# Start reordered, two chunks masked by products, six weight pieces rounded on GpSimd instead of thirteen

## The chip, the core and the metric

The kernel runs on one core of a Trainium2 chip. The core has five engines that each work through their own list in order: TensorE (PE, matrix products), VectorE (DVE), ScalarE (ACT), GpSimd (POOL) and SyncE (SP), which here issues every transfer. An instruction waits until what it needs is there, and whatever stands behind it on its engine waits with it. The metric is the device time of one execution in microseconds, as the median of the runs shown.

## The reference

Three stages follow one another on 3072 tokens (4 batches of 768) of width 256. The first is a chunked linear attention with decay, in chunks of 32 tokens:

```python
for c in range(seq // chunk):
    cum = np.cumsum(log_a[:, :, sl], axis=-1)
    L = np.exp(cum[..., :, None] - cum[..., None, :]) * causal
    M = einsum('bhin,bhjn->bhij', C, B) * L
    y[:, :, sl] = einsum('bhij,bhjd->bhid', M, x) + einsum('bhin,bhnd->bhid', C, state) * exp(cum)
    state = decay_full * state + sum(B x decay_from_j)
...
g = relu(x @ w_in) ** 2          # 256 -> 2048
x = g @ w_out                    # 2048 -> 256
...
h = (x @ w1) * (x @ w2) @ w3     # 256 -> 1024 -> 1024
out = h @ w_out                  # 1024 -> 256
```

## The kernel before

The tokens go through in tiles of 512. A tile's two feed-forward stages are phases: A (the squared relu) has 16 steps m, B the bilinear one. The order of phases is A0, A1, B0, B1 and on. The attention of a tile, five or six chunks g in units u of a few chunks, is put into slots of the phase before; only the first tile's (chunks 0 to 5, units 0 to 2) stands alone ahead of A0, in an order that is written out by hand in `startup`.

Products keep float32 accuracy by three passes: each operand is split into a high part, rounded (on ScalarE, or for weights on GpSimd), and a low part (VectorE, `split_lo`, L141), and six matmuls of 128x512 make one product. A step m of phase A is `h_mm` (first product, L816), relu (L830) and square (L838 on ScalarE or L840 on VectorE), the high part of gp (ScalarE, L846), its low part (VectorE, L141), and the second product into acc (TensorE, L863), which comes one or two steps after the first one. Names in the rows follow these tiles: mm for first products, tmp, gp, acc, xt for the attention's result, which is the operand of the next phase A.

While A0 runs, the 16 weight pieces "a" arrive (ua) and are converted: `conv_words` on ScalarE (L196, L198), `conv_bits` on VectorE (L207, L210), and `conv_parts`, which makes wa: the high part by a cast on ScalarE (L230) for pieces 0 to 2 and on GpSimd (L228) for the others, and the low part on VectorE. Pieces of the later weights (uo, cv, wo, wo2l and u3) follow on the same lines.

In the attention a chunk's e (exponentials of decays) is made by `unit_e1` on TensorE and ScalarE for units 0 to 3, from the products of `pick` (L665). For units 0 to 2 the causal mask is added by a product of ident and nmask (L660). For unit 3, which is chunks 6 and 7, `chunk_mask` cuts it afterwards with an affine select on GpSimd (L556), as it does for the chunks after them. `chunk_g` multiplies e by g (VectorE, L621), `chunk_y` makes y on TensorE (L752), the state is updated by L714, and `chunk_hand` copies it on as xb (L721). `unit_split` splits B and C of a unit, writes them to memory (hl_d) and `unit_bc` reads them back as bt and cb.

Buffers decide what waits. The pool gp has four places that are used in turn by pick (twice), zero, the gp tiles of the steps m, and the tile hl of a unit's split when it is given no other place, which is so for unit 5:

```python
def new_gp():
    return gp.tile([P, 2, 512], F32R, tag="gp", name="gp")
...
hl = wts.tile([P, 2, 512], F32R, tag=place, name="hl") if place else new_gp()
```

A tile that takes over a place waits until the readers of the former tile are done, transfers too. A transfer counts as done when it has landed. SP's transfers use eight semaphores in turn (DMAHW0 to 7), so each also waits until the one eight places ahead of it has landed. The matmuls that make up a step are emitted by a planner that sets the order on each engine by costs and by due slots; outside `startup` that order is not written down anywhere in the code.

## Time and profile before

| what | before |
|---|---|
| median of 3 runs | 561.94 us (561.61 to 562.13) |
| profiled execution's own time | 561.75 us |
| span of its records | 560.0 us |
| TensorE busy | 546.9 us, 98% of the span |
| VectorE, ScalarE, GpSimd busy | 361.9, 288.7, 88.6 us |
| granted TensorE clock over the span | 0.996 of full |
| transfers | 59.49 MB |

Times of rows are counted from the start of the span. TensorE's share is an average: the first 90 us, with the first tile's attention and the conversion of weights, are looser than the rest. Nearly all of the stalls of the run lie there and in the move to the next phases.

### The profile page before, as it was taken

The page shows a single profiled execution, that of the slowest core. Times are in us where ns is not written, and L with a number is a line of the kernel's source. Part 1 is how long each engine was busy: PE and PEld are TensorE (multiplying, and loading weights), DVE is VectorE, ACT ScalarE, POOL GpSimd, SP SyncE. Part 2 cuts the span into 40 slices and gives each one's busy share as a digit, 9 for nine tenths or more (in the row PEclk, how much of TensorE's full clock was granted, in tenths as well). Part 3 has the DMA queues.
Part 4 walks back from the last instruction along what each step waited for, and adds up shares of the span by engine and source line. Part 5 has one row for each costly group of instructions (what it writes and reads, how often), then busy time and mean ns, then how long its engine had stood idle before and what let it go on. Part 6 is the DMA issues. An engine that isn't in the chain of part 4 may idle for free.

```text
span 560.0 us, 9614 instructions
## 1 busy us (share of the span) xinstructions
PE 546.9 (98%) x3580; PEld 460.3 (82%) x3580; DVE 361.9 (65%) x655; ACT 288.7 (52%) x553; POOL 88.6 (16%) x136
## 2 busy tenths in 40 slices
PE   8979999999999999999999999999999999999997
PEld 6757777888888888888888888888888888888886
DVE  5799998977898555466476456474456574545431
ACT  6799768787884342444343444342535332544332
POOL 8264730000001240013030003020012010000000
PEclk9989999999999999999999999999999999999999
DMA  8797690253446470075250066020162220100001
GB/s 240 248 288 249 213 389 7 74 153 107 156 149 169 102 198 1 15 191 143 58 142 1 29 165 148 22 78 1 52 175 77 57 68 1 39 1 1 1 1 37
DMA packets 48735, 59.49 MB, mean 106 GB/s; under 512 B 22960, under 2 KB 36784, under 8 KB 48688
## 3 DMA queue, kind: packets, MB, share of 16 engines
q1 hardware_dynamic: 48688, 58.88, 35.5%
q8 instruction: 28, 0.46, 0.4%
q14 instruction: 19, 0.16, 0.1%
HBM read 50.20 MB, written 8.65 MB: 105 GB/s over the span
## 4 chain that ended last, share of the span: by engine, by line
PE 81%; DVE 8%; DMA 5%; ACT 3%; SPq 1%; issue 1%; DVEq 0%; ACTq 0%
PE mm L816 43%; PE acc L863 18%; PE acc L916 12%; PE mm L257 4%; PE y L752 2%; DVE gp L141 2%; PE g L615 2%; DMA hl_d<-gp 1%; DMA hl_d<-hl 1%; SPq L93 1%; DVE wa L141 1%; DMA raw<-in_raw_dram 1%; DVE cvs L207 1%; DMA u<-in_w_dram 1%; DVE cvs L210 1%
## 5 line engine op out<-in xcount | busy, mean ns | idle before, releaser
L816 PE MATMUL mm<-xt,wa 128*128 128x512 f32 x576 | 148.6, 396 | 3.2 <-DVE wa L141 2.0
L846 ACT CAST gp<-tmp 128x512 fp32r<-128x512 f32 x144 | 89.4, 621 | 115.3 <-DVE tmp L904 63.6
L863 PE MATMUL acc<-gp,wa 128*128 128x512 f32 x576 | 145.9, 392 | 1.3 <-DVE gp L141 0.7
L141 DVE TENSOR_TENSOR gp<-tmp,gp 128x512 fp32r<-128x512 f32 x144 | 103.6, 720 | 61.1 <-ACT gp L846 60.8
L816 PE MATMUL mm<-x,w 128*128 128x512 f32 x576 | 142.6, 393 | 0.0
L816 PEld LDWEIGHTS mm<-xt,wa 128*128 128x128 f32 x576 | 106.4, 190 | 25.8 <-ACT tmp L830 2.4
L863 PEld LDWEIGHTS acc<-gp,wa 128*128 128x128 f32 x576 | 106.5, 188 | 24.5 <-DVE gp L141 1.5
L816 PEld LDWEIGHTS mm<-x,w 128*128 128x128 f32 x576 | 104.5, 188 | 20.5 <-ACT tmp L896 0.2
L830 ACT ACTIVATE tmp<-mm 128x512 f32<-128x512 f32 x96 | 57.3, 596 | 50.8 <-PE mm L816 50.4
L916 PEld LDWEIGHTS acc<-w3o,gp 128*128 128x128 f32 x576 | 75.8, 190 | 4.6 <-DVE gp L141 0.3
L916 PE MATMUL acc<-w3o,gp 128*128 128x256 f32 x576 | 78.5, 283 | 0.1
L840 DVE TENSOR_TENSOR tmp<-tmp 128x512 f32<-128x512 f32 x68 | 47.5, 699 | 29.8 <-ACT tmp L830 28.5
L904 DVE TENSOR_TENSOR tmp<-tmp,mm 128x512 f32<-128x512 f32 x48 | 32.9, 686 | 48.5 <-PE mm L816 44.9
L556 POOL TENSOR_SCALAR_AFFINE_SELECT e<-e 96x768 f32<-96x768 f32 x26 | 25.8, 1005 | 235.8 <-DMA e<-e_d 228.7
L896 ACT COPY tmp<-mm 128x512 f32<-128x512 f32 x48 | 28.1, 586 | 45.9 <-PE mm L816 45.6
L575 POOL TENSOR_TENSOR xb<-xb,dec 96x256 f32<-96x256 f32 x32 | 23.1, 723 | 94.6 <-DMA xb<-in_xb_dram 93.6
L621 DVE TENSOR_TENSOR e<-g,e 128x384 f32<-128x384 f32 x52 | 27.6, 551 | 6.0 <-PE g L615 4.7
L257 PE MATMUL mm<-wo,w 128*128 128x256 f32 x128 | 23.7, 284 | 0.9 <-DVE w L141 0.9
L257 PEld LDWEIGHTS mm<-wo,w 128*128 128x128 f32 x128 | 20.6, 191 | 2.5 <-DVE w L141 1.5
L742 DVE SCALAR_TENSOR_TENSOR xb<-xb,through,y 32x64 f32<-32x64 f32 x72 | 20.4, 283 | 2.8 <-PE y L714 1.1
L615 PEld LDWEIGHTS g<-cb,bt 96*128 96x128 f32 x96 | 16.1, 190 | 2.8
L257 PE MATMUL mm<-wo2l,w 128*128 128x256 f32 x64 | 18.1, 283 | 0.0
(109 smaller groups left out, 447.2 us busy)
## 6 DMA issues: line engine op xcount, KB each, us to landing
u<-in_w_dram SPq DMA_DIRECT2D x24, 512.0 KB, 4.4
ua<-in_w_dram SPq DMA_DIRECT2D x16, 512.0 KB, 6.8
e<-e_d SPq DMA_DIRECT2D x40, 192.0 KB, 4.6
xb<-in_xb_dram SPq DMA_DIRECT2D x32, 192.0 KB, 3.7
bt<-hl_d SPq DMA_DIRECT2D x78, 48.0 KB, 2.0
hl_d<-gp SPq DMA_DIRECT2D x9, 384.0 KB, 2.5
cb<-hl_d SPq DMA_DIRECT2D x66, 48.0 KB, 2.0
out_dram<-tmp SPq DMA_DIRECT2D x10, 256.0 KB, 2.9
```

The costliest lines, as they stand in the source:

```text
L141: return nc.vector.tensor_tensor(out=lo, in0=src, in1=hi.bitcast(F32), op=ALU.subtract)
L257: nc.tensor.matmul(acc[:, :DM], v[:, l, e % 4 * P:(e % 4 + 1) * P], wo2[1 + e // 2][r][:, e % 2 * DM:(e % 2 + 1) * DM], start=(n == 0), st ...
L615: nc.tensor.matmul(ps[:, 2 * pp:2 * pp + 2], w, un["c2"][:, pr, :, j * CH:(j + 1) * CH], start=True, stop=True)
L621: nc.vector.tensor_tensor(out=m, in0=ps, in1=m, op=ALU.mult)
L816: i = nc.tensor.matmul(ps, w[m][:, l, col + k * P:col + (k + 1) * P], rhs[k][:, r, :], start=((l, r, k) == (1, 0, 0)), stop=((l, r, k) == ...
L830: nc.scalar.activation(r, ps, AF.Relu)
L840: nc.vector.tensor_tensor(out=g32, in0=r, in1=r, op=ALU.mult)
L846: nc.scalar.copy(g[:, 0, :], d[k])
L863: i = nc.tensor.matmul(acc["x2", t][e], wa[m][:, l, 256 + e * P:256 + (e + 1) * P], g[:, r, :], start=(m == 0 and n == 0), stop=(m == MF - ...
L896: nc.scalar.copy(s, ps)
L904: nc.vector.tensor_tensor(out=p32, in0=prods[t, m], in1=ps, op=ALU.mult)
L916: i = nc.tensor.matmul(acc["o"][sub // per][:, sub % per, :], g[:, l, sub * P:(sub + 1) * P], w3o[m // 2][:, r, m % 2, :], start=(m == 0 a ...
```

## The change

Four things are changed. The high part of pieces 9 to 15 is rounded on ScalarE and no longer on GpSimd. Chunks 6 and 7 are masked by the product of ident and nmask in `unit_e1`, in A0's slots 1 and 2, and no longer by `chunk_mask`. Since ident is then read during A0, it can't lie any longer where weight piece 9 will be put (wa9); it takes a place in the pool gp, after the two picks and ahead of zero. And in `startup` piece 0 is loaded ahead of chunks 4 and 5, its words are made ahead of state(2), its bits and unit 2's e, g0 and m0 come sooner.

```diff
--- before.py
+++ after.py
@@ -48,6 +48,7 @@
 NEVER = -30000.0
 WARM = 2
 CONV0 = 3
+HI_POOL = range(3, 9)
 TMPB = 6
 SQ_DVE = {0: (), 1: (3, 4, 5, 6)}
 GM_DVE = (0,)
@@ -224,7 +225,7 @@
             wo2.append(w)
             return
         w = wts.tile([P, 2, 512], F32R, tag=PLACE[j % 8] if kind == "3" else f"w{kind}{j}", name=f"w{kind}{j}")
-        if kind == "a" and j > 2:
+        if kind == "a" and j in HI_POOL:
             nc.gpsimd.tensor_copy(w[:, 0, :], v)
         else:
             nc.scalar.copy(w[:, 0, :], v)
@@ -276,7 +277,7 @@
     id2 = const.tile([P, 32], F32, name="id2")
     e_d = dram.tile([4, 2, 2, 8, H, CH], F32, name="e_d")
     pick = [gp.tile([P, H, P], F32R, tag="gp", name="pick") for k in range(2)]
-    ident = wts.tile([P, P], F32R, tag="wa9", name="ident")
+    ident = gp.tile([P, P], F32R, tag="gp", name="ident")
     nmask = act1.tile([P, P], F32R, tag="cmask", name="nmask")[:, :CH]
     m_rel = new_tmp()
     m_oth = new_tmp()
@@ -649,21 +650,20 @@
         for j, g in enumerate(UNITS[u]):
             es[g] = e[:, j] if u != 2 else None
 
-    def unit_e1(u, q, mask=True):
+    def unit_e1(u, q):
 
         if u not in e0:
             unit_e0(u)
         k, v = divmod(UNITS[u][0], 4)
         ps = new_mm()[:, :4 * CH]
         ph = ps.rearrange("p (h c) -> p h c", h=2)
-        if mask:
-            nc.tensor.matmul(
-                ps.rearrange("p (n i) -> p n i", n=4), ident, nmask.unsqueeze(1).to_broadcast([P, 4, CH]),
-                start=True, stop=False, skip_group_check=True,
-            )
+        nc.tensor.matmul(
+            ps.rearrange("p (n i) -> p n i", n=4), ident, nmask.unsqueeze(1).to_broadcast([P, 4, CH]),
+            start=True, stop=False, skip_group_check=True,
+        )
         for h in range(2):
             nc.tensor.matmul(
-                ph[:, h], pick[k][:, 2 * q + h], e_first[:, v:v + 2], start=not mask, stop=True, skip_group_check=True
+                ph[:, h], pick[k][:, 2 * q + h], e_first[:, v:v + 2], start=False, stop=True, skip_group_check=True
             )
         nc.scalar.activation(
             e0[u][q // 2][:, :, 2 * (q % 2):2 * (q % 2) + 2].rearrange("p j h i -> p h j i"),
@@ -1015,15 +1015,16 @@
         for j, s in enumerate(ASLOT):
             g = FIRST[1] + j
             put(ph, s, chunk_pre, g)
-            put(ph, s, chunk_mask, g)
+            if j > 1:
+                put(ph, s, chunk_mask, g)
             put(ph, s + 1, chunk_g, g, 0)
             put(ph, s + 1, chunk_g, g, 1)
             put(ph, s + 2, chunk_y, g)
         put(ph, 1, unit_bc, 4, BCPLACE)
         put(ph, 1, conv_load, 2)
         for s in range(2):
-            put(ph, 1 + s, unit_e1, 3, 2 * s, False)
-            put(ph, 1 + s, unit_e1, 3, 2 * s + 1, False)
+            put(ph, 1 + s, unit_e1, 3, 2 * s)
+            put(ph, 1 + s, unit_e1, 3, 2 * s + 1)
         put(ph, 4, unit_e, 4)
         put(ph, 7, unit_split, 5)
         put(ph, 10, unit_bc, 5)
@@ -1068,9 +1069,9 @@
         batch_load(1, 1, 3)
         chunk_xb(2)
         chunk_xb(3, "w124")
+        conv_load(1)
         chunk_xb(4, "w125")
         chunk_xb(5, "w126")
-        conv_load(1)
         unit_load(4)
         conv_load(2)
         picks, rounded = constants()
@@ -1107,6 +1108,7 @@
         unit_e1(1, 3)
         unit_pad(2)
         unit_g0(1)
+        conv_words(0)
         state(2)
         chunk_pre(4)
         m0(1)
@@ -1116,18 +1118,17 @@
         chunk_xb(6)
         unit_e1(2, 0)
         unit_e1(2, 1)
-        conv_words(0)
+        conv_bits(0)
+        unit_e1(2, 2)
         state(3)
+        unit_e1(2, 3)
+        unit_g0(2)
         chunk_pre(5)
         value(2)
-        unit_e1(2, 2)
-        unit_e1(2, 3)
-        conv_bits(0)
-        unit_g0(2)
+        m0(2)
         state(4)
         value(3)
         decays_e(0)
-        m0(2)
         conv_load(1)
         unit_load(5)
         conv_parts(0)
```

Three places show what this moves in the engines' lists. The first is ScalarE in the middle of A0, where the steps m6 and m7 get the high parts of their gp tiles (gp_938 and gp_983 before, gp_940 and gp_985 after; ua10 to ua12 are weight pieces, xb_541 takes over the state for one of the next chunks). Before:

```order
L846 CAST gp_938<-tmp_889 128x512 [waits Activation_49]
L196 ACTIVATE cvs_88<-ua11_632 128x512 [waits DMAHW3_49,DVE_49]
L198 ACTIVATE ua11_632<-ua11_632 128x512
L838 ACTIVATE tmp_936<-tmp_916 128x512 [waits Activation_49]
L144 CAST xt1_773<-y_105 128x96 [waits DVE_49]
L846 CAST gp_983<-tmp_936 128x512 [waits DMAHW2_49,DMAHW1_49,Activation_49]
L196 ACTIVATE cvs_87<-ua12_730 128x512 [waits DMAHW0_49,Pool_49]
L198 ACTIVATE ua12_730<-ua12_730 128x512
L721 COPY xb_541<-y_105 32x256 [waits DVE_49]
```

And after:

```order
L846 CAST gp_940<-tmp_891 128x512 [waits DMAHW2_49,DMAHW1_49,Activation_49]
L197 ACTIVATE cvs_88<-ua11_632 128x512 [waits DMAHW3_49,Pool_49]
L199 ACTIVATE ua11_632<-ua11_632 128x512
L838 ACTIVATE tmp_938<-tmp_918 128x512 [waits Activation_49]
L231 CAST wa9_902<-cvs_87 128x512 [waits DVE_49]
L721 COPY xb_541<-y_105 32x256 [waits DVE_49]
L846 CAST gp_985<-tmp_938 128x512 [waits Activation_49]
L197 ACTIVATE cvs_87<-ua12_733 128x512 [waits DMAHW0_49,Pool_49]
L199 ACTIVATE ua12_733<-ua12_733 128x512
L231 CAST wa10_949<-cvs_88 128x512 [waits DVE_49]
```

The waits for two transfers (DMAHW1 and DMAHW2) stand on the cast of m7 before and on that of m6 after, one step sooner; three casts L231 of weight pieces are new. On SP, these two semaphores at that point of the program belong to the writing of unit 5's split, whose tile is gp_746 after; the order of transfers around it is that of before:

```order
L94 DMA ua12_733<-in_w_dram 128x1024 [waits DMAHW0_49]
L94 DMA hl_d5_751<-gp_746 128x2x96 [waits DMAHW1_49,DVE_49]
L94 DMA hl_d5_751<-gp_746 128x2x96 [waits DMAHW2_49,DVE_49]
L94 DMA ua13_800<-in_w_dram 128x1024 [waits DMAHW3_49]
L94 DMA xb_809<-in_xb_dram 96x512 [waits DMAHW4_49]
L94 DMA bt_90<-hl_d5_751 32x4x96 [waits DMAHW5_49,DMAHW1_49,PE_49]
```

The second place is TensorE at the end of A0 (wa12 to wa15 are the last pieces, xt1 the operand of A1, xb_881 and xb_883 belong to chunk 10). Before:

```order
L752 MATMUL y_105<-e_876,xb_881 32x96 x8
L714 MATMUL y_105<-xb_881,pb_1092 32x64 x4
L714 MATMUL y_105<-xb_1001,pb_1069 32x64 x4
L863 MATMUL acc_713<-gp_1243,wa14_1132 128x512 x3
L863 MATMUL acc_714<-gp_1243,wa14_1132 128x512 x3
L816 MATMUL mm_1246<-xt1_772,wa0_511 128x512
L816 MATMUL mm_1296<-xt1_772,wa1_579 128x512
L816 MATMUL mm_1316<-xt1_772,wa2_599 128x512
L863 MATMUL acc_713<-gp_1263,wa15_1183 128x512 x2
L863 MATMUL acc_714<-gp_1263,wa15_1183 128x512 x2
L863 MATMUL acc_713<-gp_1263,wa15_1183 128x512
L863 MATMUL acc_714<-gp_1263,wa15_1183 128x512
```

And after:

```order
L863 MATMUL acc_716<-gp_1265,wa15_1185 128x512 x2
L863 MATMUL acc_717<-gp_1265,wa15_1185 128x512 x2
L863 MATMUL acc_716<-gp_1265,wa15_1185 128x512
L863 MATMUL acc_717<-gp_1265,wa15_1185 128x512
L752 MATMUL y_105<-e_878,xb_883 32x96 x8
L714 MATMUL y_105<-xb_883,pb_1094 32x64 x4
L714 MATMUL y_105<-xb_1003,pb_1071 32x64 x4
L816 MATMUL mm_1248<-xt1_775,wa0_511 128x512
L816 MATMUL mm_1298<-xt1_775,wa1_579 128x512
L816 MATMUL mm_1318<-xt1_775,wa2_599 128x512
L816 MATMUL mm_1248<-xt1_776,wa0_511 128x512
L816 MATMUL mm_1248<-xt1_775,wa0_511 128x512
```

Before, chunk 10's y and states stand ahead of the second products of m14 and m15, and m15's stands between three matmuls of A1 and the rest of A1. After, chunk 10's y follows the last second product, and A1 follows that.

The third place is VectorE there, after the low part of m15's gp (gp_1265), up to the low part of xt1_775 (e_878 is chunk 10's e; cv and wo2l are later weights, x2 is the result of A0):

```order
L208 SCALAR_TENSOR_TENSOR cv_1279<-cv_1279,uo2_1041 128x512 [waits Activation_49]
L142 TENSOR_TENSOR xt1_776<-y_105,xt1_776 128x96 [waits Activation_49]
L721 COPY xb_883<-y_105 32x256
L622 TENSOR_TENSOR e_878<-g_1109,e_878 128x384 [waits DMAHW7_49,Pool_49]
L622 TENSOR_TENSOR e_878<-g_1113,e_878 128x384
L211 SCALAR_TENSOR_TENSOR cv_1268<-uo1_992,cv_1268 128x512 [waits DVE_49]
L211 SCALAR_TENSOR_TENSOR cv_1279<-uo2_1041,cv_1279 128x512 [waits DVE_49]
L142 TENSOR_TENSOR x2_1333<-acc_716,x2_1333 128x512 [waits Activation_49]
L142 TENSOR_TENSOR x2_1336<-acc_717,x2_1336 128x512 [waits Activation_49]
L142 TENSOR_TENSOR wo2l_1276<-cv_1268,wo2_1275 128x512 [waits Activation_49]
L208 SCALAR_TENSOR_TENSOR cv_1288<-cv_1288,uo3_1089 128x512 [waits Activation_49]
L142 TENSOR_TENSOR xt1_775<-y_105,xt1_775 128x64 [waits Activation_49]
```

Before, the part of xt that is 64 wide stood ahead of m15's low part and of x2:

```order
L141 TENSOR_TENSOR xt1_772<-y_105,xt1_772 128x64 [waits Activation_49]
L141 TENSOR_TENSOR gp_1263<-tmp_1241,gp_1263 128x512 [waits Activation_49]
L207 SCALAR_TENSOR_TENSOR cv_1266<-cv_1266,uo1_990 128x512 [waits Activation_49]
L206 TENSOR_SCALAR u36_1399<-u36_1399 128x512 [waits DMAHW0_49]
L207 SCALAR_TENSOR_TENSOR cv_1277<-cv_1277,uo2_1039 128x512 [waits Activation_49]
L141 TENSOR_TENSOR xt1_773<-y_105,xt1_773 128x64 [waits Activation_49]
L210 SCALAR_TENSOR_TENSOR cv_1266<-uo1_990,cv_1266 128x512 [waits DVE_49]
L210 SCALAR_TENSOR_TENSOR cv_1277<-uo2_1039,cv_1277 128x512 [waits DVE_49]
L141 TENSOR_TENSOR x2_1331<-acc_713,x2_1331 128x512 [waits Activation_49]
L141 TENSOR_TENSOR x2_1334<-acc_714,x2_1334 128x512 [waits Activation_49]
```

So the cast and the low part of xt1_776, which go after xt1_775's, have moved behind x2's low parts.

## Rows read from the trace of the kernel before

**Rows 1.** Busy time of each engine in stretches of the span (instruction counts in brackets).
```profile
25.90:56.10 30.20, 26.18 (x132) 20.62 (x133) 28.81 (x46) 28.97 (x60) 15.08 (x19) 0.94 0.87 265
56.10:82.49 26.39, 25.42 (x167) 19.46 (x165) 26.39 (x43) 17.90 (x35) 16.41 (x20) 1.00 0.83 296
```

**Rows 2.** Timeline of TensorE, 25 to 45: start, length, idle before with releaser.
```profile
29.40 1.61 PE L816 MATMUL mm<-xt,wa 128*128 128x512 f32 x6 [1.46 <-DVE wa L141]
...
34.84 0.84 PE L665 MATMUL mm<-e_first,pick 128*128 128x192 f32 x4 [1.39 <-ACT e L668]
...
44.10 1.16 PE L816 MATMUL mm<-xt,wa 128*128 128x512 f32 x4 [0.56 <-DVE wa L141]
```

**Rows 3.** Timeline of TensorE, 56 to 93, two stalls and their neighbour.
```profile
55.66 1.61 PE L863 MATMUL acc<-gp,wa 128*128 128x512 f32 x6
...
70.69 0.54 PE L752 MATMUL y<-e,xb 128*32 128x96 f32 x16 [0.62 <-DVE xt L141]
...
77.59 1.21 PE L863 MATMUL acc<-gp,wa 128*128 128x512 f32 x4 [0.25 <-ACT gp L846]
```

**Rows 4.** Timeline of TensorE, 81 to 93, the end of A0.
```profile
82.49 1.52 PE L816 MATMUL mm<-xt,wa 128*128 128x512 f32 x6
83.85 0.61 PE L863 MATMUL acc<-gp,wa 128*128 128x512 f32 x2
84.72 0.54 PE L752 MATMUL y<-e,xb 128*32 128x96 f32 x16 [0.25 <-DVE e L621]
...
85.73 1.65 PE L863 MATMUL acc<-gp,wa 128*128 128x512 f32 x6
...
89.26 3.56 PE L816 MATMUL mm<-xt,wa 128*128 128x512 f32 x15
```

**Rows 5.** Busy windows around the half-clock stretch (PEclk is the granted clock).
```profile
33.10:36.50 3.40, 1.99 (x12) 1.45 (x11) 3.40 (x6) 3.40 (x9) 3.15 (x5) 1.00 1.03 368
36.50:39.90 3.40, 3.40 (x10) 2.66 (x8) 3.00 (x4) 3.31 (x7) 3.25 (x5) 0.50 1.03 338
```

**Rows 6.** Chain that ended last, 41 to 61: start, length, what.
```profile
48.09 7.97 DMA hl_d<-gp
```

**Rows 7.** Timeline of ScalarE, 52.4 to 60.
```profile
53.26 0.61 ACT L846 CAST gp<-tmp 128x512 fp32r<-128x512 f32 x1
...
56.48 0.62 ACT L846 CAST gp<-tmp 128x512 fp32r<-128x512 f32 x1 [0.47 <-DMA hl_d<-gp]
```

**Rows 8.** Timeline of ScalarE, 12 to 26.
```profile
16.05 0.36 ACT L721 COPY xb<-y 32x256 f32<-32x256 f32 x1 [0.94 <-PE y L714]
```

**Rows 9.** GpSimd's groups by line, 25 to 84: count, busy us, mean ns, idle before.
```profile
L228 POOL CAST wa<-cvs 128x512 fp32r<-128x512 f32 x13 | 12.1, 933 | 28.1 <-ACT wa L230 14.1 <-DVE cvs L210 2.8 <-ACT xt L144 2.7
...
L556 POOL TENSOR_SCALAR_AFFINE_SELECT e<-e 96x768 f32<-96x768 f32 x5 | 5.2, 1048 | 0.3
```

**Rows 10.** Timeline of VectorE, 46 to 63.
```profile
47.37 1.36 DVE L207 SCALAR_TENSOR_TENSOR cvs<-cvs,ua 128x512 uint32<-128x512 uint32 x1
...
61.65 1.01 DVE L621 TENSOR_TENSOR e<-g,e 128x384 f32<-128x384 f32 x2
```

**Rows 11.** Timeline of VectorE, 81 to 93.
```profile
83.18 0.43 DVE L721 COPY xb<-y 32x256 f32<-32x256 f32 x1
83.64 1.02 DVE L621 TENSOR_TENSOR e<-g,e 128x384 f32<-128x384 f32 x2
...
86.92 0.69 DVE L141 TENSOR_TENSOR gp<-tmp,gp 128x512 fp32r<-128x512 f32 x1 [0.25 <-ACT gp L846]
...
89.20 1.28 DVE L210 SCALAR_TENSOR_TENSOR cv<-uo,cv 128x512 uint32<-128x512 uint32 x2
```

**Rows 12.** Timeline of TensorE, 92 to 140, its longer stalls.
```profile
101.52 2.11 PE L863 MATMUL acc<-gp,wa 128*128 128x512 f32 x8 [0.43 <-DVE gp L141]
...
121.30 0.51 PE L257 MATMUL mm<-wo,w 128*128 128x256 f32 x2 [0.88 <-DVE w L141]
```

## The prediction

> **What bounds the kernel now.** I read the busy windows first. Between 56.10 and 82.49 us TensorE is busy for 25.42 of 26.39 us, and the stretch ahead of it, from 25.90, has 26.18 of 30.20 [rows 1]: what TensorE gets, in its own order, is the time. From 92 us on the changed kernel's rows are those of before on every engine, so all that the change can move lies ahead of that. I then read TensorE's timeline for its stalls. At the start of phase A0 it idles 1.46 us (released by VectorE's weight piece) and 1.39 us (by ScalarE's e), and 0.56 at 44.10 [rows 2]. After 56 us the timeline shows 0.62 at 70.69, 0.25 at 77.59 and 0.25 at 84.72 [rows 3, 4]. In 36.50 to 39.90 the granted clock is 0.50, the lower level of 1.2 GHz, after 3.40 us in which TensorE was busy for 1.99; ten matmuls start there [rows 5]. At a full-clock pitch of 0.227 us (six L816 from 82.49 to 83.85 [rows 4]) 3.40 us hold 15 to 16, so this stretch costs about 1.3 us. Last I read the chain that ended last: around 50 us it hangs on one transfer, hl_d<-gp, issued at 48.09 and landed 7.97 us later [rows 6]; ScalarE's cast L846 of 56.48 waits 0.47 us for it [rows 7].
>
> **The start.** The reordered start puts piece 0's words into ScalarE's idle 0.94 us ahead of 16.05 [rows 8], so its bits and unit 2 come sooner. Bounds: 0, and 0.9 us for the start of A0; I take 0.8. The transfers of chunks 4 and 5 move one place back, by less than 1 us, and their readers stand several chunks later. Four mask products (384 columns each, under 0.227 us of TensorE a piece) lie where TensorE idles 1.46 and 1.39 us [rows 2]: nothing on the path, at most 0.9.
>
> **GpSimd, VectorE, ScalarE.** Seven of the 13 casts L228 (0.933 us each) and two of five selects (1.048) leave GpSimd [rows 9]. Beside a select, L207 took 1.36 us [rows 10], where a plain VectorE operation of that size took 0.69 [rows 11]; two L621 of 61.65, read from PSUM, took 1.01 together, unstretched [rows 10, 11]. At 0.25 to 0.68 us a piece, nine removals give VectorE some 3 us back. The Trainium skill (SBUF — State Buffer, section on the two separate sides) says that VectorE and GpSimd hold their shared port pair as an exclusive lock, the loser being blocked for a whole instruction. By that rule up to 8.6 us would come back; the rows show partial stretching, and this case's trace bears the rule out only in part. TensorE can gain from it only its stalls: 0.62 and 0.25 here [rows 3], 0.56 at 44.10 [rows 2], by either reading. ScalarE gets seven casts of 0.62 us (as L846 [rows 7]), 4.3 us, against 26.39 - 17.90 = 8.5 us of its idle time [rows 1]: hidden, as long as it isn't held.
>
> **The shared buffers: where I see the price.** The gp ring has four places. Ident now takes one, ahead of zero, and this moves which step of A0 inherits the place of unit 5's split, whose data the transfer hl_d<-gp reads. Before, it was the step m7: its cast L846 is the one at 56.48. The one of m6 had run at 53.26 [rows 7]. After, in the order on ScalarE, the cast of m6 (gp_940) carries the two DMA waits and that of m7 has none. I expect the landing at its old time: the loads ahead of it are the same, in the same order on SP, and the transfer of 7.97 us stands behind weight loads, not behind computing [rows 6]. So ScalarE stops at this cast until 56.48. Behind it there stand piece 11's words, m7's square, piece 9's cast (now on ScalarE), the hand-over xb and m7's cast; VectorE waits for m6's high part, and TensorE for both.
>
> Step m6's second product began as the third matmul of the group at 55.66, at 55.66 + 2 x 0.227 = 56.1 [rows 3]. After, not before 56.48 + 0.62 = 57.1: **1.0 us later**, whatever the start has gained. A start 0.8 sooner, 0.56 less at 44.10 and VectorE's relief would have brought TensorE there at 54.1 to 55.3; all of that becomes idle time, 1.8 to 3.0 us in one piece. This is the step that I trust most.
>
> **From there to A1.** Before, 26.39 us lie between 56.10 and the last first product, h15, at 82.49 [rows 1, 4]. In the new order six second products (1.36 us) and chunk 9's y with its state stand behind h15. Chunk 10's y with two states took 84.72 to 85.73, 1.01 us [rows 4]; I estimate chunk 9's at 0.9. If the 0.62 and 0.25 go too, h15 starts at 57.1 + 26.39 - 1.36 - 0.9 - 0.87 = 80.4 and ends at T = 81.7.
>
> The tail is new. Before, chunk 10's y stood ahead of m14's products, and m15's second product between the first three matmuls of A1 and the rest at 89.26 [rows 4]. After, all second products come first, then y(10), then A1. TensorE's own work from T to that rest is 0.9 + 20 x 0.227 + 1.01 + 3 x 0.227 = 7.1 us. VectorE's in-order list is longer. Before, m15's low part started at 86.92 [rows 11], 3.1 us after h15 ended at 83.85 [rows 4], partly since ScalarE was busy; I take 2.6. Behind it, at 0.6 us a full operation (two in 1.28 [rows 11]), there stand two L208, one shift (0.4), xt (0.2), xb (0.43), two e (1.0 [rows 11]): e is ready at T + 6.5, where TensorE has come to y(10) at T + 5.4. Then two L211, x2's two low parts, wo2l, L208 and xt_775's low part: 6 x 0.6 + 0.2 more, to T + 10.3. Only then is ScalarE's cast of xt_776 allowed (0.2), which the rest of A1 needs. So A1's rest starts at T + 10.5 less what overlaps: I take T + 10.2 = 91.9, **2.6 us later** than 89.26; bounds +1.6 (the list starts when h15 ends, and half the 0.6s are hidden) and +3.3.
>
> VectorE has then done work that it did later before. TensorE's stalls of 0.43 at 101.52 (VectorE's gp) and 0.88 at 121.30 (VectorE's w) [rows 12] can shrink: bounds 0 and 1.3; I take 0.4, most of the nearer one. Sum, against the profiled execution's own 561.75 us (span 560.0): 561.75 + 2.6 - 0.4 = 563.95, say **564.0 us**. The median of the runs shown is 0.19 above that execution, within what I call no change: 0.2%, 1.1 us, about what a measurement of this kernel can tell, 560.8 to 563.1.
>
> **The clock.** An idle stretch of 1.39 us was followed by the half clock, one of 1.46 us wasn't [rows 2, 5]. The change makes one of 1.8 to 3.0 us and, in the tail, about 3 us in two or three pieces. Bounds: 0 and 2 x 1.3. I keep it out of the sum and give it a chance. The Trainium skill (TensorE: Matmul & The Clock Gate, on the HAM clock gate) ties the half rate to an array that has been idle. By that rule alone a partly busy stretch would cost nothing; the trace differs, since the clock fell after TensorE had been busy for 1.99 of 3.40 us.
>
> **The rivals.**
> 1. *As summed, full clock*: 564.0 us, 563.1 to 564.7. Chance 0.40.
> 2. *The wait of m6 or the tail is followed by a half-clock stretch*, as at 36.50 [rows 5]: + 1.3 once, 565.3; twice 566.6. For it: TensorE's pauses are longer than those that preceded it before. Against: the 1.46 us at 29.40 had no such end. Chance 0.27.
> 3. *The tail costs little*, since VectorE reaches m15's low part sooner or what it does early comes back in full at 101.52 and 121.30: 561.75 + 1.6 - 1.3 = 562.0, 561.2 to 563.1. Chance 0.17.
> 4. *The other side: hl_d<-gp isn't what m6 waits for.* If it lands before TensorE gets there, at about 54 us, the start's gain stays: 3.0 us less than in the sum (1.0, and 2.0 of 0.8, 0.56 and VectorE's relief), 561.0; with VectorE's relief passed on to 101.52 and 121.30 (0.9 more), 560.1. I set 560.4, and it decides at a landing 2.4 us sooner than 56.4. For it: the split's inputs may be ready sooner. Against: the transfer stands behind weight loads that land one after the other. By the lock rule of the Trainium skill named above the relief would be larger, and this end likelier. Chance 0.15.
> That the change doesn't do what it says is excluded by the order: the casts are on ScalarE, the selects gone.
>
> **How the numbers follow.** Faster is case 4, with 0.01 of case 3: 0.15 in all. Case 3 is no change for 0.16, and 0.02 of case 1 ends there: 0.18. The rest, 0.67, is slower. The range goes from case 4, 560.4, to 566.2, between one half-clock stretch and two; it leaves out about 0.08 below and 0.08 above.
>
> **What would show it.** ScalarE's cast L846 of m6 starts within 0.2 us of the landing of hl_d<-gp, with an idle time ahead of it of more than 1 us, and TensorE has an idle stretch of 1.8 to 3.0 us just ahead of the second product of m6, around 57 us; the start of A0 lies near 25.1; h15 starts near 80.4; A1's rest starts between 91 and 92.6, with idle time released by VectorE's e and ScalarE's xt ahead of it; the windows show a half clock after 57 us or not. If TensorE passes m6 before 56 us, the step on the gp ring is wrong, and with it the sign. If A1's rest starts before 90.5, the tail is mis-sized.

## The result, and the profile after

The changed kernel takes 568.91 us (median of 20 runs, 564.75 to 572.01), the kernel before, beside it on the same chip, 562.34 us (20 runs, 561.53 to 565.99). The ratio is 1.011, with a 95% interval of 1.009 to 1.0129: slower, as forecast, but by 6.6 us and not by 2, and above the range. The profiled execution took 568.79 us, with a span of 567.1 us, 7.1 more than before.

I read TensorE's timeline from 25 to 100 us first, the same view as [rows 2 to 4]. Its longer stalls in the changed kernel (left out are 1.09 and 1.39 us at the start of A0, near to those of before, and 1.18 at 42.38 for a high part of gp):

```profile
26.97 1.66 PE L816 MATMUL mm<-xt,wa 128*128 128x512 f32 x6 [0.88 <-ACT xt L145]
...
58.07 1.72 PE L863 MATMUL acc<-gp,wa 128*128 128x512 f32 x4 [1.79 <-ACT gp L846]
81.13 1.86 PE L816 MATMUL mm<-xt,wa 128*128 128x512 f32 x6 [2.09 <-DVE wa L142]
93.62 0.54 PE L752 MATMUL y<-e,xb 128*32 128x96 f32 x16 [0.83 <-issue]
95.49 0.96 PE L816 MATMUL mm<-xt,wa 128*128 128x512 f32 x3 [0.78 <-ACT xt L145]
97.55 2.78 PE L816 MATMUL mm<-xt,wa 128*128 128x512 f32 x11 [1.10 <-ACT xt L145]
```

The row at 58.07 is the second product of m6, that at 81.13 the first product of step 14 (h14), that at 93.62 chunk 10's y, that at 97.55 the rest of A1. Before, of these last five places only chunk 10's y had a stall, 0.25 us [rows 4]. h15 stands between them; from a closer look at the same timeline:

```profile
85.35 1.78 PE L816 MATMUL mm<-xt,wa 128*128 128x512 f32 x6
```

Four busy windows between these marks, and two around the half clock (the column behind POOL is the granted clock), show where the 7.1 us went:

```profile
26.97:58.07 31.10, 25.29 (x136) 19.87 (x136) 26.61 (x47) 27.04 (x58) 15.11 (x21) 1.00 0.86 259
58.07:85.35 27.28, 25.19 (x135) 19.91 (x135) 23.52 (x42) 23.57 (x47) 5.12 (x6) 0.88 0.87 300
85.35:97.55 12.20, 9.49 (x86) 7.03 (x84) 10.09 (x21) 7.17 (x16) 1.14 (x2) 0.98 0.06 24
97.55:567.10 469.55, 465.77 (x2857) 397.61 (x2857) 280.94 (x505) 216.23 (x400) 42.02 (x60) 1.00 0.28 78
...
58.53:61.94 3.41, 3.41 (x10) 2.62 (x9) 3.14 (x7) 3.36 (x8) 1.42 (x2) 0.50 0.30 72
82.42:85.83 3.41, 3.41 (x10) 2.63 (x9) 3.13 (x8) 3.08 (x6) 0.00 (x0) 0.50 0.96 383
```

Set against the steps of the prediction (the predicted end of the records is 564.0 less the 1.75 us by which the time of before stands over its span):

| mark | before | predicted | after | after less predicted, from mark to mark |
|---|---|---|---|---|
| second product of m6 | 56.1 | 57.1 | 58.07 | +0.97 |
| h15 | 82.49 | 80.4 | 85.35 | +3.98 |
| rest of A1 | 89.26 | 91.9 | 97.55 | +0.70 |
| end of the records | 560.0 | 562.25 | 567.1 | -0.80 |

The sum is +4.85. The largest part, 3.98, lies between m6 and h15. TensorE waits 2.09 us there for the low part of piece 14, and its clock is at the half rate of 1.2 GHz from 58.53 to 61.94 and from 82.42 on. The half clock of before, at 36.50 [rows 5], is gone from this execution.

Why piece 14 is late stands in VectorE's timeline from 68 to 82 us:

```profile
72.65 0.43 DVE L207 TENSOR_SCALAR uo<-uo 128x512 uint32<-128x512 uint32 x1 [2.39 <-DMA uo<-in_w_dram]
72.99 0.69 DVE L208 SCALAR_TENSOR_TENSOR cvs<-cvs,ua 128x512 uint32<-128x512 uint32 x1
74.47 0.43 DVE L207 TENSOR_SCALAR uo<-uo 128x512 uint32<-128x512 uint32 x1 [0.79 <-DMA uo<-in_w_dram]
74.81 0.69 DVE L142 TENSOR_TENSOR wa<-cvs,wa 128x512 fp32r<-128x512 f32 x1
...
78.02 1.36 DVE L208 SCALAR_TENSOR_TENSOR cvs<-cvs,ua 128x512 uint32<-128x512 uint32 x1
...
80.40 0.68 DVE L142 TENSOR_TENSOR wa<-cvs,wa 128x512 fp32r<-128x512 f32 x1
```

The shift of uo, the first piece of a weight that A0 doesn't need, now stands ahead of piece 14's bits in VectorE's list. VectorE gets to it at 70.26, before its transfer has landed (72.62), and waits 2.39 us; the first half of the bits (72.99) waits with it. The shift of a second piece of that weight waits 0.79 us more, ahead of the second half of the bits (75.41). The low part at 80.40 is what h14 waited for. Before, the first shift came behind both halves, and its transfer had been there since 69.76:

```profile
71.42 0.68 DVE L210 SCALAR_TENSOR_TENSOR cvs<-ua,cvs 128x512 uint32<-128x512 uint32 x1
...
73.64 0.84 DVE L206 TENSOR_SCALAR uo<-uo 128x512 uint32<-128x512 uint32 x1
```

### The profile page after: what moved, and what is told of

Its sections match the earlier page's. It is cut to its first block, busy times and chain, and to the rows that moved or that the text cites. A ratio compares the mean times of both kernels' runs of the same rounds, so it can differ in the third digit from the quotient of the medians.

```text
span 567.1 us, 9609 instructions
## 1 busy us (share of the span) xinstructions
PE 549.2 (97%) x3584; PEld 462.6 (82%) x3584; DVE 356.8 (63%) x655; ACT 292.0 (52%) x560; POOL 78.5 (14%) x127
## 4 chain that ended last, share of the span: by engine, by line
PE 83%; DVE 6%; DMA 5%; ACT 4%; issue 1%; SPq 1%; DVEq 0%; ACTq 0%
PE mm L816 43%; PE acc L863 19%; PE acc L916 12%; PE mm L258 4%; PE y L752 2%; PE g L616 2%; DMA uo<-in_w_dram 1%; DMA hl_d<-gp 1%; SPq L94 1%; DMA raw<-in_raw_dram 1%; DVE e L676 1%; DMA u<-in_w_dram 1%; DVE gp L142 1%; DVE cv L208 1%; ACT gp L846 1%
## 5 line engine op out<-in xcount | busy, mean ns | idle before, releaser
L863 PE MATMUL acc<-gp,wa 128*128 128x512 f32 x576 | 147.5, 395 | 3.3 <-ACT gp L846 3.3
L142 DVE TENSOR_TENSOR gp<-tmp,gp 128x512 fp32r<-128x512 f32 x144 | 102.3, 711 | 68.0 <-ACT gp L846 67.5
L557 POOL TENSOR_SCALAR_AFFINE_SELECT e<-e 96x768 f32<-96x768 f32 x24 | 23.3, 984 | 235.1 <-DMA e<-e_d 232.9
L622 DVE TENSOR_TENSOR e<-g,e 128x384 f32<-128x384 f32 x52 | 27.7, 552 | 5.6 <-PE g L616 4.3
```

The source lines that it names most:

```text
L142: return nc.vector.tensor_tensor(out=lo, in0=src, in1=hi.bitcast(F32), op=ALU.subtract)
L622: nc.vector.tensor_tensor(out=m, in0=ps, in1=m, op=ALU.mult)
L863: i = nc.tensor.matmul(acc["x2", t][e], wa[m][:, l, 256 + e * P:256 + (e + 1) * P], g[:, r, :], start=(m == 0 and n == 0), stop=(m == MF - ...
```

## The experiments

Three causes were open after this: the shared gp buffers (m6's wait), the casts on ScalarE as such, and the order that the moved casts give to VectorE's list. Each kernel was timed in five rounds beside the kernel before, whose median was 562.0 to 562.5 us in every batch.

### The parts one by one

**e1** puts ident back where it was; everything else of the change stays.

```diff
-    ident = gp.tile([P, P], F32R, tag="gp", name="ident")
+    ident = wts.tile([P, P], F32R, tag="wa9", name="ident")
```

> The changed kernel with ident back in the place of weight piece 9; nothing else differs, and the cast of m7, not of m6, now waits for unit 5's transfer. Theory 1 (the shared gp place): ScalarE's 3.2 us wait at m6 and TensorE's 1.8 us in front of m6's second product go, and with them the half clock after 58 us; 2 to 4 us faster than the changed kernel's 568.9, near 565 to 567, as VectorE's wait for uo and the tail stay. Rival (the transfer's late landing only moves the wait on, since m7 follows 2.3 us later): within 1 us of the changed kernel. Rival (the half clock comes with a phase of its own): time unchanged in the median, only the stretch differs.

Measured: 567.89 us (6 runs), ratio 1.0095 [1.0076, 1.0114]. The wait at m6 is gone, and A1's rest starts at 93.82 and not at 97.55. Yet only 1.0 us of the time comes back, less than theory 1's 2 to 4, and the intervals overlap with those of the whole change. TensorE now waits 1.30 and 2.09 us for weight pieces, 0.89, 0.79 and 0.83 us at the end of A0, and its clock is at half from 92.31 to 99.14. From its timeline:

```profile
73.34 1.67 PE L816 MATMUL mm<-xt,wa 128*128 128x512 f32 x6 [1.30 <-DVE wa L142]
...
78.91 1.65 PE L816 MATMUL mm<-xt,wa 128*128 128x512 f32 x6 [2.09 <-DVE wa L142]
...
93.82 6.17 PE L816 MATMUL mm<-xt,wa 128*128 128x512 f32 x15 [0.83 <-ACT xt L145]
```

The 15 matmuls from 93.82 took 6.17 us, where those of before took 3.56 [rows 4]: most of the 3.73 us that A1's rest came sooner was lost there.

**e2** is e1 with all 13 casts on GpSimd, so that only the masks and the new start remain.

```diff
-HI_POOL = range(3, 9)
+HI_POOL = range(3, 16)
```

> The changed kernel with ident in the place of weight piece 9 and all 13 pieces rounded on GpSimd again; it keeps the masks by products and the new start. Theory 1 (VectorE, relieved of GpSimd's casts, reaches the shift of uo before its weights land and holds wa14 back, 2.1 us at h14 and a half clock behind it): the wait goes or shrinks below 0.5 us, 563 to 565. Rival (the list order, uo's shift ahead of piece 14's second half, does it alone, as it stands here too): VectorE still waits over 1 us for uo, and the time is that of e1.

Measured: 563.23 us (12 runs), 1.0025 [1.0007, 1.0043]. That is 4.7 us less than e1 beside it, so the casts carry most of the price. The time is theory 1's, but the wait that was to go is the rival's: VectorE waits for uo here too, and TensorE for a weight piece behind it (VectorE, then TensorE):

```profile
72.33 0.43 DVE L207 TENSOR_SCALAR uo<-uo 128x512 uint32<-128x512 uint32 x1 [2.88 <-DMA uo<-in_w_dram]
```

```profile
73.41 2.75 PE L816 MATMUL mm<-xt,wa 128*128 128x512 f32 x6 [2.09 <-DVE wa L142]
```

With this wait the kernel is only 1.3 us over the one before; the end of A0 has no stall over 0.43 us.

**e3** is the changed kernel with the `startup` of before.

```diff
-        conv_load(1)
         chunk_xb(4, "w125")
         chunk_xb(5, "w126")
+        conv_load(1)
...
-        conv_words(0)
         state(2)
...
```

> The changed kernel with the start order of before. Theory 1 (the start is not what costs: what it gains or loses ahead of m6 is swallowed by the wait there): within 1 us of 568.9. Rival (piece 0's load ahead of chunks 4 and 5 takes bandwidth from unit 1's raw data, VectorE's pad and e come 1 us later, and A0 starts 1.1 us later): A0 starts at about 25.9, as before, and the time is 1 to 1.5 us below the changed kernel.

Measured: 568.42 us (6 runs), 1.0097 [1.0064, 1.0129]: the start is not the cause.

**e4** is the kernel before with the seven casts moved and nothing else.

```diff
+HI_POOL = range(3, 9)
...
-        if kind == "a" and j > 2:
+        if kind == "a" and j in HI_POOL:
```

> The kernel before with pieces 9 to 15 rounded on ScalarE; nothing else. Theory 1 (VectorE relieved of GpSimd's casts, TensorE's stalls of 0.62, 0.25 and 0.25 go; uo's shift stands behind piece 14 in this order, so VectorE doesn't wait long for it): 0 to 1.5 us faster than 562.3, 561 to 562.3. Rival (the cast on ScalarE alone brings the tail's order and uo's wait): 1 to 3 us slower.

Measured: 568.18 us (4 runs), 1.0102 [1.0083, 1.0121]: +6.2 us, as much as the whole change without any of its other parts. **e8**, the kernel before with only the masks by products, took 561.94 us (12 runs), 0.9992 [0.9978, 1.0005]; **e9**, with only the new start, 562.25 us (11 runs), 0.9995 [0.9985, 1.0004]. Their edits are the hunks of `unit_e1` with `chunk_mask`, and of `startup`, of the change.

> The kernel before with chunks 6 and 7 masked by products, ident left in the place of weight piece 9; nothing else. Theory 1 (the mask products lie in idle time and cost nothing; VectorE gains 1.2 us beside the two selects that go; the shift of uo now stands between piece 14's halves): 0 to 1.5 us slower than 562.0, by VectorE's wait for uo. Rival (the masks pay): 0.5 to 1.5 us faster.

> The kernel before with the new start order alone. Theory 1 (piece 0's load ahead of chunks 4 and 5 delays unit 1's raw data, and A0 starts 0.3 to 1 us later; nothing behind it takes that back or adds to it): 562.5 to 563.5, 0 to 1 us slower. Rival (as I forecast: A0 starts 0.8 us sooner): 0.5 to 1 us faster.

Neither moves the time by more than the noise, though I had expected up to 1.5 us for e8 and up to 1 us for e9. Together, in e2, they cost a little. VectorE's list around uo is the same in e8 and e2, and the new start is what e2 adds. Its uo landed at 72.30, in e8 at 69.11, and VectorE's wait for it was 2.88 us against 0.60, in one profile of each.

### Where e4's time goes

In e4 TensorE has done all products of A0 at 86.51 (90.80 - 4.29), where before they ended only ahead of 89.26 [rows 4], and loses it in one place. Timeline of TensorE, and of VectorE ahead of it:

```profile
90.80 0.87 PE L753 MATMUL y<-e,xb 128*32 128x96 f32 x16 [4.29 <-issue]
93.03 6.30 PE L817 MATMUL mm<-xt,wa 128*128 128x512 f32 x18 [0.30 <-ACT xt L145]
```

```profile
86.39 0.24 DVE L142 TENSOR_TENSOR xt<-y,xt 128x96 fp32r<-128x96 f32 x1
86.56 1.28 DVE L211 SCALAR_TENSOR_TENSOR cv<-uo,cv 128x512 uint32<-128x512 uint32 x2
87.76 1.28 DVE L142 TENSOR_TENSOR x<-acc,x 128x512 fp32r<-128x512 f32 x2
88.96 0.24 DVE L142 TENSOR_TENSOR xt<-y,xt 128x96 fp32r<-128x96 f32 x1
89.22 0.43 DVE L722 COPY xb<-y 32x256 f32<-32x256 f32 x1
89.68 1.02 DVE L622 TENSOR_TENSOR e<-g,e 128x384 f32<-128x384 f32 x2
```

The releaser reads "issue", so the profile names nobody. But chunk 10's e ends at 89.68 + 1.02 = 90.70, and TensorE starts 0.10 us later; in the rows of e5, e14, e15 and of the changed kernel the distance is 0.10 or 0.11 as well. VectorE has had the piece ahead (xt, 0.24) in hand at 86.39, and then works 2.4 us on bits of the output weight and on the low parts of x2 (x<-acc, called residual adds in the expectations below), for which no stall of TensorE shows here. From 90.28 to 97.11 the clock is at half. The kernel before had its one half-clock stretch in A0 at 36.50 [rows 5]; e4 has that one too (from 35.67).

Two attempts to repair this by holding instructions in their written place (`keep`) failed.

**e5** is e4 with m15's second product held in its written place.

```diff
-                x2_mm(t, m)
+                x2_mm(t, m, fixed=t == 0 and m > 14)
```

> The kernel before with pieces 9 to 15 rounded on ScalarE (as e4), and with the second product of m15 kept behind chunk 10's y in TensorE's list. Theory 1 (the casts' price is the order at the end of A0: TensorE idles 4.3 us for chunk 10's e, and the clock falls behind it): the idle time in one piece falls below 2 us, the half clock of 90 to 97 us goes, and the time is 562 to 564 instead of e4's 568.2. Rival (chunk 10's e itself is late, since VectorE waits for uo and chunk 9's y is late): the idle time moves ahead of m15's second product with the same length, and the time stays near 567 to 568.

Measured: 568.33 us (6 runs), 1.0121 [1.009, 1.0152]. TensorE waits 4.47 us ahead of chunk 10's y, from VectorE's e at 89.96. It is e that is late, wherever TensorE's products stand.

**e6** is the changed kernel with the shift of uo held, and with it the second half of the bits of pieces 14 and 15.

```diff
-            nc.vector.tensor_single_scalar(lo_w, lo_w, 29, op=ALU.logical_shift_right)
+            k = keep if kind == "o" else (lambda x: x)
+            k(nc.vector.tensor_single_scalar(lo_w, lo_w, 29, op=ALU.logical_shift_right))
...
+        k = keep if kind == "a" and j > 13 else (lambda x: x)
+        k(nc.vector.scalar_tensor_tensor(
```

> The changed kernel, in which VectorE's shift of piece uo is kept behind the bits of weight pieces 14 and 15. Theory 1 (VectorE's wait for uo's landing costs 2.1 us at h14 and brings the half clock of 82 us): that wait and the stall at h14 go; 2 to 3.5 us faster than 568.9, 565.5 to 567. Rival (the tail is bound by VectorE's list from m15 on, and swallows what is gained before): h14 comes sooner, but the idle time of the tail grows by as much; within 1 us of 568.9.

Measured: 569.9 us (4 runs), 1.0134 [1.0114, 1.0154]. The time is the rival's, within 1 us of the changed kernel, but not by way of the tail. The stall at h14 shrank to 1.28 us, and VectorE's wait only changed its name. VectorE's waits from 25 to 100 us (total, times, longest) begin so:

```profile
DVE u L208 <- DMA u<-in_w_dram: 5.9, 3, 4.2
DVE gp L142 <- ACT gp L848: 5.8, 5, 4.3
```

A later weight's piece, u, took uo's place, and the wait at m6 was 3.27 us long. Work that VectorE had put off came back as stalls of TensorE in A1 (0.77 and 0.75 us, both for a low part of gp). **e7** has all three repairs, ident of e1, the holds of e6 and that of e5:

> The changed kernel with ident in the place of weight piece 9, uo's shift behind pieces 14 and 15, and m15's second product behind chunk 10's y. Theory 1 (three waits and the half clocks behind them are the price): 561 to 563, at or below the kernel before. Rival (the casts on ScalarE cost for another reason): above 565.

Measured: 566.06 us (6 runs), 1.0073 [1.005, 1.0096]. A third to a half of the loss comes back (by the ratio, or by 3.6 us over before and not 6.6), not all of it as theory 1 had it. Waits of 1.42 us for a weight piece and 1.13 us ahead of chunk 10's y are still there.

**e10** to **e12** hold the shifts of all later weights and chunk 10's e, in e4, in e1 and, as a control, in the kernel before.

```diff
+            k = keep if kind != "a" else (lambda x: x)
+            k(nc.vector.tensor_single_scalar(lo_w, lo_w, 29, op=ALU.logical_shift_right))
...
+        k = keep if g == 10 else (lambda x: x)
+        k(nc.vector.tensor_tensor(out=m, in0=ps, in1=m, op=ALU.mult))
```

> The kernel before with pieces 9 to 15 rounded on ScalarE (as e4), and with VectorE's shifts of the later weights (uo, u) and chunk 10's e kept in the order of the program, so that these shifts no longer run ahead. Theory 1 (with the casts gone from GpSimd the later weights' conversions move ahead in VectorE's list, wait there for their transfers and hold back the chain xt, xb, e of chunks 9 and 10): no wait of VectorE for uo or u before A0 ends, TensorE's 4.3 us idle time falls below 2 us, and the time is 562 to 564.5. Rival (the price lies in ScalarE's casts being late for wa): 567 to 569, with TensorE released by VectorE's wa.

> The changed kernel with ident in the place of weight piece 9 and the same hold as e10. Theory 1: both causes gone, 562 to 564 with the new start in it. Rival: above 565, as e7.

> The kernel before with the same hold as e10, as a control: the hold itself. Theory 1: within 1 us of before, since the shifts didn't wait long there. Rival (the hold costs in A1, where the later weights come later): 1 to 3 us slower, which would then be part of e10 and e11 too.

Measured: 576.22 (5 runs), 574.6 (6 runs) and 574.08 us (4 runs), 1.0247, 1.0215 and 1.0199, far outside what theory 1 had for any of them. The control alone costs 2%, some 11 us, with a new wait behind A1's products:

```profile
107.44 0.80 PE L258 MATMUL mm<-wo,w 128*128 128x256 f32 x2 [3.39 <-DVE w L141]
```

The casts add 2.1 us in place of 6.2 on top of it. That points at the list, but the hold moves so much that I don't call it shown. A better test changes the list without holding anything.

### Three, four and five of the casts

Which casts move changes VectorE's list in different ways. In the order of the programs, with nothing run, chunk 10's hand-over stood as before with pieces 9 to 12 on ScalarE, as in e4 with 11 to 15, and in between with 13 to 15. The stretch of VectorE's list around that hand-over (xt, xb, e x2), for e13 and e4:

```
e13: xt, xt, xb, e x2, wo2l, u, gp, cv, cv, xt, cv, u, cv, x, x
e4:  wo2l, gp, cv, u, cv, xt, cv, cv, x, x, xt, xb, e x2
```

So a price for each cast and a price of the list order these kernels differently. In the expectations, theory A is the list and theory B a price for each cast on ScalarE.

```diff
+HI_POOL = (3, 4, 5, 6, 7, 8, 13, 14, 15)
...
-        if kind == "a" and j > 2:
+        if kind == "a" and j in HI_POOL:
```

This is e13's edit; e14 has `range(3, 11)` there, e15 `range(3, 13)`.

> The kernel before with four of the seven casts moved: pieces 9 to 12 on ScalarE, 3 to 8 and 13 to 15 on GpSimd. In VectorE's list chunk 10's hand-over (xt, xt, xb, e) stands ahead of the output weight's second and third piece and ahead of the residual adds, as in the kernel before. Theory A (the list's order costs): 562 to 563.5, no idle time of TensorE over 1.5 us at the end of A0, no half clock there. Theory B (each cast on ScalarE costs, +6.2 for seven): 4/7 of it, 565.5 to 566.

> The kernel before with five of the seven casts moved: pieces 11 to 15 on ScalarE. In VectorE's list chunk 10's hand-over stands behind the bits of the output weight's second and third piece and behind the first residual add, as with all seven moved. Theory A: 566.5 to 568.5, with 3 to 5 us idle on TensorE ahead of chunk 10's product and a half-clock stretch behind it. Theory B: 5/7 of 6.2, 566.5 to 567. So this run alone does not part the two; beside the runs with three and four casts it does.

> The kernel before with three of the seven casts moved: pieces 13 to 15 on ScalarE. In VectorE's list chunk 10's hand-over stands behind the first half of the bits of the output weight's second and third piece (about 1.4 us of work), but ahead of the second half and the residual adds. Theory A: between the two, 564 to 567, and over the run with four casts by 1.5 or more. Theory B: 3/7 of 6.2, 564.5 to 565.2, and under the run with four casts.

| kernel | casts moved | measured | over before | interval of the ratio |
|---|---|---|---|---|
| e13 | 4 | 563.18 us (12 runs) | +0.9 | 1.0001 to 1.0043 |
| e15 | 3 | 564.88 us (7 runs) | +2.6 | 1.0029 to 1.0068 |
| e14 | 5 | 568.65 us (6 runs) | +6.4 | 1.0093 to 1.0135 |
| e4 | 7 | 568.18 us (4 runs) | +6.2 | 1.0083 to 1.0121 |

Four cost less than three, and five as much as seven: the time follows the list and not the number. e13 and e15 lie in theory A's ranges, e14 0.15 us above its own. e15's time lies in theory B's range too; it is the order of e13 and e15, and the time of e14, that B can't give. TensorE's timeline at the end of A0 gives the same order, for e13, e15 and e14 in turn:

```profile
89.81 3.69 PE L817 MATMUL mm<-xt,wa 128*128 128x512 f32 x15 [0.42 <-ACT xt L145]
```

```profile
87.48 0.54 PE L753 MATMUL y<-e,xb 128*32 128x96 f32 x16 [0.73 <-issue]
89.37 0.96 PE L817 MATMUL mm<-xt,wa 128*128 128x512 f32 x3 [0.80 <-ACT xt L145]
91.75 5.23 PE L817 MATMUL mm<-xt,wa 128*128 128x512 f32 x15 [1.42 <-ACT xt L145]
```

```profile
90.71 0.87 PE L753 MATMUL y<-e,xb 128*32 128x96 f32 x16 [3.89 <-issue]
92.93 5.19 PE L817 MATMUL mm<-xt,wa 128*128 128x512 f32 x18 [0.30 <-ACT xt L145]
```

Idle time ahead of chunk 10's y and of A1 is 0.42, 2.95 and 4.19 us. On VectorE, chunk 10's e starts at 84.27, 86.36 and 89.58. The clock is at half from 90.74 to 94.15 in e14 and from 91.64 to 95.06 in e15; in e13 it isn't at the end of A0. A price of certain casts, those of pieces 13 to 15, could explain e13 and e15, but then e4 would cost about 0.9 + 2.6 = 3.5 us; it costs 6.2.

**e16** is e13 with the masks by products. In its list the hand-over stands as before, but uo's shift stands ahead of piece 14's bits, as in the changed kernel.

> The kernel before with the masks of chunks 6 and 7 by products (identity where it was) and pieces 9 to 12 on ScalarE. Chunk 10's hand-over stands in VectorE's list ahead of the output weight's second and third piece, as before; the shift of the output weight's first piece stands ahead of piece 14's bits, as in the changed kernel. Theory A, with the hand-over deciding: 561.5 to 563.5. If the shift's place decides: 564 to 566, with VectorE waiting over 2 us for the landing and TensorE for piece 14. Theory B: 565 to 566.

Measured: 565.18 us (6 runs), 1.0043 [1.0026, 1.0061]. By time alone that is theory B's figure too; the trace tells what it is. The wait is for uo, as expected, but it reached TensorE mainly through gp and not through piece 14. VectorE, then TensorE:

```profile
71.30 0.43 DVE L207 TENSOR_SCALAR uo<-uo 128x512 uint32<-128x512 uint32 x1 [3.96 <-DMA uo<-in_w_dram]
```

```profile
75.19 1.22 PE L863 MATMUL acc<-gp,wa 128*128 128x512 f32 x2 [3.15 <-DVE gp L142]
77.03 2.93 PE L816 MATMUL mm<-xt,wa 128*128 128x512 f32 x6 [0.61 <-DVE wa L142]
```

The wait for uo is there by itself, held up a low part of gp and so TensorE for 3.15 us, and the clock fell:

```profile
74.77:81.60 6.83, 5.80 (x13) 4.12 (x14) 6.83 (x13) 1.71 (x4) 3.23 (x4) 0.50 1.03 410
```

At the end of A0 no stall over 0.25 us is left. So the list has two places that cost, each seen without the other: uo's shift ahead of weight bits that are needed sooner (e16, +2.9 over before, +2.0 over e13, which lacks it), and the hand-over behind later weights (e14, +6.4). The changed kernel has some of both. How its 6.6 us divide between them and the wait at m6 isn't shown: e1, e6 and e7 took single waits away, and others came in their place.

No kernel here beats the one before: the best, e8, is within the interval of no change.

## Why the prediction was right in sign and too small

**GpSimd, VectorE, ScalarE.** The casts were hidden on ScalarE, as I wrote: e13 has four of them there at 0.9 us in all. VectorE's busy time fell from 361.9 to 356.8 us, by 5.1 where I took 3; but in e1, with the same casts and selects gone, it fell to 358.9, by 3.0, so one profile doesn't fix the figure. The Trainium skill (SBUF — State Buffer, section on the two separate sides) has VectorE and GpSimd exclude one another for whole instructions, by which I had worked out up to 8.6; it says this of VectorE operations in a two-port mode or with two inputs in SBUF. The single rows agree with it, and my "partial stretching" was a misreading. L208 at 78.02 took 1.36 us, since it ended at 79.38, 0.55 after this select on GpSimd (at 78.83):

```profile
77.77 1.06 POOL L557 TENSOR_SCALAR_AFFINE_SELECT e<-e 96x768 f32<-96x768 f32 x1
```

L211 at 75.41 and the L142 at 76.45 also ended 0.55 us after the GpSimd operation beside them, close to the 0.68 that such an operation takes alone. The L621 that I set against this have an operand in PSUM. The step that failed here is the sentence that TensorE can gain from the relief "only its stalls". It left out that relief also rearranges VectorE's list, and that TensorE can lose by that. e4 shows that this loss by itself can be as large as that of the whole change; in the changed kernel it falls in other places.

**The shared buffers.** The mechanism was right. ScalarE's timeline has the cast of m6 as written down:

```profile
57.40 0.62 ACT L846 CAST gp<-tmp 128x512 fp32r<-128x512 f32 x1 [3.23 <-DMA hl_d<-gp]
```

The 1.79 us in which TensorE stands lie at the low end of my 1.8 to 3.0, and that is luck: TensorE came there at 56.28 and not at 54.1 to 55.3, and the transfer came 0.9 us later than I had it. "I expect the landing at its old time" failed. The split is written by two transfers, and the cast waits for both. The second one, in the chain that ended last:

```profile
50.12 7.18 DMA hl_d<-gp
```

It landed at 57.30. The row of [rows 6] is the first of the two; the second was issued at 48.58 and landed at 56.38 before. So it was issued 1.54 us later and landed 0.92 later, and the cast started 0.92 later (57.40 against 56.48): that is nearly all of the 0.97 us of the first mark. On SP the piece load just ahead of it came later by as much (49.18 against 47.61): the same loads in the same order, but not at the same time. Why they were late isn't settled; A0 as a whole began 1.09 us later than before. As a price of its own the ring is small (e1, 1.0 us, intervals overlapping), since TensorE reaches the next places sooner without it and then waits there (e1's 1.30 us for a weight piece is new).

**The start.** I took 0.8 us sooner; A0 began at 26.97, later than the 25.88 of before. e9 (26.33, same time as before within 0.1%) and e3 show that this has no price of its own. In company it may have a small one: uo landed 3.19 us later in e2 than in e8. The landing moves without the new start as well, though: it was at 71.3 in e16.

**From there to A1.** This is the step that failed most. "If the 0.62 and 0.25 go too, h15 starts at 80.4" assumed that nothing new would stop TensorE between m6 and h15. The order of the changed list had uo's shift ahead of piece 14's bits, and I hadn't asked when VectorE would get there and what stands behind it. The old landing, 69.76, against the 70.26 at which VectorE got there would still have shown no wait: uo landed 2.86 us later than before, 1.27 by its issue and 1.59 by a longer transfer. VectorE's waits of 2.39 and 0.79 us became 2.09 on TensorE, and half clock (58.53 to 61.94, and from 82.42 on) did about the rest of the +3.98.

The tail that I worked out was right in kind and nearly in size: chunk 10's y and A1 wait for VectorE's e and for xt, the stalls of 0.83, 0.78 and 1.10 us make 2.71, and the stretch from h15 to A1's rest is 0.70 us longer than predicted. The credit in A1 was too small. From A1's rest to the end it was 469.55 us against 470.74 before, 1.2 us less, where I took 0.4 of a bound of 1.3.

**The clock.** "I keep it out of the sum" failed. Rival 2 happened twice, with 566.6 us as its time, one half-clock stretch after the wait at m6 and one after that at h14. With the wait for piece 14, 2.09 us, 566.6 becomes 568.7, and the profiled execution took 568.79. The agreement is partly luck, since the smaller errors of the table cancel. A stretch also costs less than my 1.3: ten products in 3.41 us take 2.27 at my pitch of 0.227, which leaves 1.1. The Trainium skill (TensorE: Matmul & The Clock Gate, on the HAM clock gate) ties the half rate to an idle array. The trace agrees in part: each of the two stretches came behind an idle time of about 2 us, but 0.46 and 1.29 us after TensorE had resumed.

**Rivals 3 and 4** are out: the tail's stalls are there, and m6 waited for the transfer that I had named. The chances of the four add up to 0.99; by them faster is 0.16 and slower 0.65, not 0.15 and 0.67.

## What to carry to other kernels

When work is taken off an engine whose list a planner writes, read the new lists of all engines before counting the gain: for each instruction that moved forward, set the landing of its data against the time at which the engine now gets there, allow for a landing that moves (uo's by 2.86 us here), and name what stands behind it. A small hand-over piece that stood behind a row of long operations, for which nobody waited yet, cost the idle time here and then the clock (e4). When several casts can be moved, try subsets, since the time follows the list that each subset makes and not their number.

## What the runs showed of the hardware

- Half-clock stretches in A0 and A1 came behind idle time, but no length of idle time parts the cases: in e1 stalls of 0.89, 0.79 and 0.83 us with short work between them were followed by half clock (92.31 to 99.14), while in the changed kernel 0.83, 0.78 and 1.10 us in the same place were not. The 2.09 us ahead of a weight piece were followed by it in e2 (73.64 to 77.05) and in the changed kernel, not in e1. In 3.41 us at half clock ten matmuls start, as before at 36.50, where 15 fit at full clock.
- Single executions of the changed kernel spread over 7.3 us and those of before over 4.5. There is one profile for each kernel, so whether half-clock stretches that come and go make this spread stays open.
- The uo transfer took 6.29 us from the end of its issue (66.33) to landing (72.62) in the changed kernel and 4.70 us before (65.06 to 69.76). Why it is slower wasn't tried.
- VectorE operations of 128x512 with two inputs in SBUF that began during a GpSimd operation ended 0.55 us after it: L211 at 75.41, L142 at 76.45 and L208 at 78.02 in the changed kernel, the last one at twice its plain 0.68 us. Two L622 at 60.97, with an operand in PSUM, took 1.01 us together beside one, no longer than elsewhere.
